# One more norm transposed by the DMA crossbar, and a new hand-written order, in a fused transformer block on one core

## The chip, the cores and the metric

The kernel runs on one core of one Trainium2 chip. The core has a matrix engine (TensorE, PE in the profile; PEld is its weight load), a vector engine (DVE), a scalar engine with activation tables (ACT), a general engine (POOL) and an engine used here to issue DMAs (SyncE, SP; SPq in the profile). The engines run side by side; each takes its own instructions strictly in order and waits on semaphores for data of the others. PSUM is the memory into which PE writes, SBUF the memory of everything else on the core. The metric is the device time of one launch in microseconds (us); lower is better. The profile is of one execution.

## The reference

One block of a transformer over 2048 tokens of width 512, all in bf16:

```python
mod = (silu(c) @ w_mod).reshape(1, 6, 1, 512)      # sa, ca, ga, sb, cb, gb
h = layernorm(x) * (1 + ca) + sa
q, k, v = heads(h @ wqkv)                          # 32 heads of 16
# each token attends to 8 tokens: itself and those 2, 4, ..., 14 before it
logits = einsum('bhsd,bhswd->bhsw', q, k[idx]) * 16 ** -0.5   # masked before token 0
o = einsum('bhsw,bhswd->bhsd', softmax(logits), v[idx])
x = x + ga * (o @ wo)
h = layernorm(x) * (1 + cb) + sb
x = x + gb * ((gelu(h @ w_gate) * (h @ w_up)) @ w_down)       # inner width 1792
```

## The kernel before

The tokens are cut into five groups: 0 and 1 have 256 tokens each, 2, 3 and 4 have 512. Each group passes through the same stages, and stages of different groups run side by side. In the profile they are known by these lines and names:

- First norm: DVE statistics (`st`, `mv`), the factor `rstd`, then `xn` (L532); a transpose puts the width on the partitions (`hT`); the modulation by `scl` and `modT` is applied after the transpose.
- qkv: PE, L673, `qkv_ps` from `hT` and `wq`, `wk`, `wv`; ACT copies the results to `qT`, `kT`, `vT` (L696). `vT` goes out to a DRAM scratch `scr` (L700) and comes back in shifted copies `vR` (L717).
- Attention: DVE multiplies q with shifted k (`pq`, L756), PE sums over the head (L768, into `LT`), ACT copies `LT` to `Lb` (L786), DVE takes a maximum in three steps (L789, L791, L793), PE subtracts it in PSUM (L798), ACT takes the exponential `e` (L805), PE sums (`ss`, L813), ACT inverts the sum by a logarithm and an exponential (L818, L819), DVE scales `e` (L822) and multiplies with `vR` (`pv`, L834 or L840), PE sums into `o_ps` (L853), ACT copies to `oT` (L859).
- Projection and second norm: PE `x_ps` (L878), DVE adds to x with a running sum (L882), ACT squares (L885), DVE and POOL make the factor `rstd` (L889, L891, L893, and the power at L537), DVE writes `xn` (L532), a transpose gives `h2T`.
- Feed-forward: PE `g_ps` and `u_ps` (L919), ACT the gelu `gl` (L928) and a copy `ub` (L931), DVE the product `hht` (L932), PE `y_ps` with the down weights `WdP` (L945), DVE adds (L953), SP stores (L956). `WdP` is multiplied by gb beforehand, in seven DVE operations (L973); `woP` by ga (L970).

A norm is transposed in one of two ways. Function `transposed` uses PE: eight 128x128 transposes for 256 tokens (L561, into PSUM `tp`), then four ACT operations that read PSUM, modulate, and write SBUF (L547). Function `crossbar` uses a transposing DMA from SBUF to SBUF, one for each 256 tokens (L583), issued by SP, and then four ACT operations that modulate in place (L593):

```python
        for half, xn in enumerate(xns):
            dma(262e3, lambda half=half, xn=xn: nc.sync.dma_start_transpose(
                out=dst[:, 2 * half:2 * half + 2, :, :].rearrange("p c d t -> p (c d) t"),
                in_=xn[:].rearrange("p i d -> p (i d)")), r=[xn], w=[(dst, ("half", half))], ...)
```

Two tables say which groups go which way: `XB1` for the first norm (group 4 by crossbar), `XB2` for the second (groups 2, 3 and 4).

The order of the work is not written out but planned when the kernel is built. Every stage records operations with an engine, an assumed duration, the tiles that they read and write, and a priority. Class `Plan` (`order`) then places one operation after another: of those whose inputs are placed it takes the one with the smallest pair of start time and priority, the start time being that at which the engine is free and the inputs have arrived, by the assumed durations. `PRI` holds the priorities: one per group for the stages ("ln1", "qkv", "att", "ffn", "glu"), one for each load ("load"), for the scratch stores and loads ("scr", "vR"), for the scaling of the weights ("wo", "wd") and the modulation rows ("mod"). `Plan.MARGIN` adds a time to an operation's start in this choice, per engine; `Plan.AHEAD` and `Plan.SKEW` say how early loads may be issued and how late they are assumed to land. These numbers decide nothing but the order of instructions on each engine.

Tiles come from rings of buffers. Those that matter here: four PSUM buffers (`psF`) for qkv, g, u and y; two (`psB`) for `x_ps`, `ss`, parts of `o_ps` and `tp`; two (`psL`) for `LT`; six for `pq` and `pv` together; three each for `gl` and `ub`; two each for `hT`, `h2T` and `vR`.

Of the kernel before, what the change touches and what calls it, by code (L numbers as in the profile page):

```python
# [184 lines left out]
class Engines:  # L185
    def __init__(self, nc, pl):
# [15 lines left out]
FMERGE = 0  # L202
CUT = 384
XB1 = {4: "act"}
XB2 = {2: "act", 3: "act", 4: "act"}
PRI = {
        "mod0": -90.9,
        "ln1": (-1628, -1309.8, -689.8, -49.3, 487.8),
        "qkv": (-615.4, 221.2, 164.3, 607.2, 1344.9),
        "att": (-458.5, 37.3, -1094.5, 559.4, 1849),  # L210
        "ffn": (1261.5, 2894.6, 2852.9, 2242.7, 1657.1),
        "glu": (-231.3, 441.7, -2194.3, 198.6, 1828.7),
        "mod": (-156.3, -280.2, 267.6),
        "wo": 978.5,
        "wd": 1221.7,
        "scr": -2870.3,
        "vR": -3349.8,
        "warm": (5, 7, 0, 3),
        "load": {"wv": -995.5, "x1": -998.36, "x2": -995.23, "wm2": -996.59, "wo": -880.76, "x3": -1009.12,
        "wm3": -995, "wm4": -996.09, "x4": -995.73, "Wg": -870.11, "Wu": -862.75, "wm5": -860.91, "Wd":  # L220
        -862.75},
}
Plan.MARGIN = {"pe": 0.45, "act": 0.17, "dve": 0.22, "pool": 0.29, "sp": -0.46}
Plan.AHEAD = 2.49
Plan.SKEW = 2
Plan.TURN = 0


# [1 line left out]
def kernel(  # L230
# [299 lines left out]
    def norm(tok, xn, i, mean, rstd, p):  # L530
        base = getattr(mean, "base", mean)
        dve(0.325, lambda: nc.vector.tensor_scalar(  # L532
            out=xn[:, i, :], in0=xrow(tok), scalar1=mean[:, i:i + 1], scalar2=rstd[:, i:i + 1], op0=ALU.subtract,
            op1=ALU.mult), r=[xkey(tok), (base, i), (rstd, i)], w=[(xn, i)], pri=p)
# [46 lines left out]
    def crossbar(xns, n, dst, off, p, on):  # L581
# [3 lines that stand above are left out]
                in_=xn[:].rearrange("p i d -> p (i d)")), r=[xn], w=[(dst, ("half", half))], pri=p, us=1.25, bw=290e3)  # L585
        for dt in range(DT):
            if on == "dve":
                dve(0.14 + n * 0.26e-3, lambda dt=dt: nc.vector.tensor_scalar(
                    out=dst[:, :, dt, :], in0=dst[:, :, dt, :], scalar1=scl[:, off // 2 + dt:off // 2 + dt + 1],
                    scalar2=modT[:, off + dt:off + dt + 1], op0=ALU.mult, op1=ALU.add),  # L590
                    r=[dst, (scl, off), (modT, off)], w=[(dst, dt)], pri=p)
            else:
                act(act_us(n, 2), lambda dt=dt: nc.scalar.activation(  # L593
                    out=dst[:, :, dt, :], in_=dst[:, :, dt, :], func=ACT.Identity,
                    scale=scl[:, off // 2 + dt:off // 2 + dt + 1], bias=modT[:, off + dt:off + dt + 1]),
                    r=[dst, (scl, off), (modT, off)], w=[(dst, dt)], pri=p)

    def columns(t, g, dt, xb):
        return t[:, :, dt, :] if g in xb else t[:, dt, 0:GROUPS[g][1]]

    def shaped(ap, g, xb):
        return ap.rearrange("p (c t) -> p c t", t=P) if g in xb else ap
# [103 lines left out]
    def emit_attention(g):  # L706
# [155 lines left out]
        lo = tok0 % SG if FMERGE else 0  # L862
        h2[g] = h2[g - 1] if lo else T("h2T", [P, n // P, DT, P] if g in XB2 else [P, DT, SG], BF16, "h2T")
        xns = []
        for half in range(n // 256):
# [31 lines left out]
            for i in range(2):  # L897
                norm(tok0 + 256 * half + P * i, xn, i, sx, rstd, p2)
        if g in XB2:
            crossbar(xns, n, h2[g], 8, base + 12, XB2[g])  # L900
        else:
            transposed(xns, n, h2[g], 8, base + 12, "ln2", ("psB", "psB"), False, lo)

    def emit_ffn(g):
# [4 lines left out]
        for u in range(units):  # L909
            p = PRI["ffn"][g] + u  # L910
            gu = []
            for Wt in (Wg, Wu):
                ps = T("psF", [P, nf, n], F32, "g_ps" if Wt is Wg else "u_ps", "ffn")

                def mm(Wt=Wt, ps=ps, u=u):
                    for f in range(nf):
                        ft = u * nf + f
                        for dt in range(DT):
                            nc.tensor.matmul(shaped(ps[:, f, :], g, XB2), lhsT=Wt[:, dt, ft * P:(ft + 1) * P],  # L919
                                             rhs=columns(h2[g], g, dt, XB2), start=(dt == 0), stop=(dt == DT - 1))  # L920

# [87 lines left out]
```

## Time and profile before

| | us |
|---|---|
| median of 4 runs (245.83 to 250.4) | 246.98 |
| the profiled execution, its own time | 246.29 |
| its span in the profile | 244.2 |
| PE busy | 236.3 |
| ACT busy | 159.9 |
| DVE busy | 158.5 |
| POOL busy | 15.7 |

The span is the time from the first to the last recorded instruction; 2.1 us of the execution's time lie around it. The busy times are sums over the span of the work of each engine. TensorE's granted clock is 0.993 over the span.

### The profile page before, as it was taken

To read this page: it belongs to the slowest core of one execution; us is meant where nothing else is said; L and a number is where in the kernel's file an instruction comes from. 1 tells how busy PE (TensorE), PEld (TensorE's weight loads), DVE (VectorE), ACT (ScalarE), POOL (GpSimd) and SP (SyncE) were. 2 spreads that over 40 slices of the span, in tenths; PEclk is the share of its full clock that TensorE was granted. 3 is DMA by queue.
4 is the path that set the end of the run, shared out by engine and by line. 5 is a ranking of instruction groups with operands and counts; after the bars stand their busy time and mean duration, and the time that the engine had idled before them with its cause. 6 is when DMAs were issued, how large, how long until landed. Compare 5 with 4: busy or idle time off the path is not lost.

```text
span 244.2 us, 4209 instructions
## 1 busy us (share of the span) xinstructions
PE 236.3 (97%) x1598; PEld 127.3 (52%) x1598; DVE 158.5 (65%) x302; ACT 159.9 (65%) x293; POOL 15.7 (6%) x37
## 2 busy tenths in 40 slices
PE   7899699999999999999999999999999999999995
PEld 2589455557675546675444444444444444444443
DVE  3569999639998699963699896369647222222222
ACT  5076897699887679478967675865767801666400
POOL 6002220100002000020000002000002000000000
PEclk9799999999999999999999999999999999999999
DMA  6999999999900129621108603101002200100011
GB/s 190 363 363 294 320 290 345 248 307 233 213 4 0 43 66 241 133 58 32 43 20 188 143 0 78 32 21 47 0 1 43 46 29 14 43 3 0 0 43 43
DMA packets 35477, 27.97 MB, mean 115 GB/s; under 512 B 9985, under 2 KB 34306, under 8 KB 35458
## 3 DMA queue, kind: packets, MB, share of 16 engines
q1 hardware_dynamic: 35456, 27.71, 44.0%
q8 instruction: 12, 0.20, 0.3%
q14 instruction: 7, 0.06, 0.1%
q10 hardware_dynamic: 2, 0.00, 0.0%
HBM read 21.40 MB, written 4.21 MB: 105 GB/s over the span
## 4 chain that ended last, share of the span: by engine, by line
PE 81%; DVE 9%; ACT 4%; DMA 2%; SPq 1%; POOL 1%; issue 1%; DVEq 0%; POOLq 0%
PE y_ps L945 18%; PE u_ps L919 18%; PE g_ps L919 18%; PE qkv_ps L673 14%; PE x_ps L878 5%; DVE pq L756 3%; PE o_ps L853 3%; DMA wm<-in_w_mod_dram 2%; DVE st L616 2%; PE LT L768 2%; ACT hT L593 1%; ACT hT L547 1%; PE LT L798 1%; POOL rstd L537 1%; DVE hht L932 1%; DVE xn L532 1%
## 5 line engine op out<-in xcount | busy, mean ns | idle before, releaser
L919 PE MATMUL u_ps<-h2T,Wu 128*128 128x512 bf16 (+1 forms) x280 | 57.7, 337 | 0.0
L919 PE MATMUL g_ps<-h2T,Wg 128*128 128x512 bf16 (+1 forms) x280 | 57.6, 336 | 0.0
L945 PE MATMUL y_ps<-WdP,hht 128*128 128x512 bf16 (+2 forms) x238 | 50.7, 367 | 0.0
L928 ACT ACTIVATE gl<-g_ps 128x512 bf16<-128x512 f32 x56 | 33.5, 599 | 22.7 <-PE g_ps L919 17.7
L932 DVE TENSOR_TENSOR hht<-gl,ub 128x512 bf16<-128x512 bf16 x56 | 23.5, 424 | 31.3 <-ACT ub L931 30.9
L931 ACT CAST ub<-u_ps 128x512 bf16<-128x512 f32 x56 | 32.7, 585 | 13.0 <-PE u_ps L919 12.7
L919 PEld LDWEIGHTS <-Wg 128*128 128x128 bf16 x280 | 27.2, 98 | 22.9 <-issue 0.6
L919 PEld LDWEIGHTS <-Wu 128*128 128x128 bf16 x280 | 27.0, 98 | 22.7 <-issue 2.1
L756 DVE TENSOR_TENSOR pq<-qT,kT 128x2048 bf16<-128x2048 bf16 x32 | 37.7, 1220 | 0.3 <-ACT kT L696 0.3
L945 PEld LDWEIGHTS <-hht 128*128 128x128 bf16 x238 | 22.7, 98 | 25.4 <-issue 0.4
L953 DVE TENSOR_TENSOR x_sg<-y_ps,x_sg 128x512 bf16<-128x512 f32 (+2 forms) x17 | 10.9, 658 | 27.3 <-PE y_ps L945 27.3
L834 DVE TENSOR_TENSOR pv<-e,vR 128x2048 bf16<-128x2048 bf16 x24 | 28.3, 1219 | 0.1
L537 POOL TENSOR_TENSOR rstd<-rstd,neghalf 128x2 f32<-128x2 f32 x14 | 11.5, 826 | 170.4 <-DVE rstd L893 106.1
L673 PE MATMUL qkv_ps<-hT,wq 128*128 128x512 bf16 (+1 forms) x80 | 17.8, 362 | 0.4 <-ACT hT L547 0.3
L673 PE MATMUL qkv_ps<-hT,wk 128*128 128x512 bf16 (+1 forms) x80 | 16.6, 340 | 0.0
L673 PE MATMUL qkv_ps<-hT,wv 128*128 128x512 bf16 (+1 forms) x80 | 15.2, 337 | 0.0
L878 PE MATMUL x_ps<-woP,oT 128*128 128x512 bf16 x64 | 15.1, 379 | 0.0
L885 ACT ACTIVATE xn<-x_sg 128x512 bf16<-128x512 bf16 x16 | 10.0, 626 | 6.9 <-DVE x_sg L882 6.7
L673 PEld LDWEIGHTS <-wq 128*128 128x128 bf16 x80 | 9.3, 119 | 6.2 <-issue 0.9
L882 DVE SCALAR_TENSOR_TENSOR x_sg<-x_ps,x_sg 128x512 bf16<-128x512 f32 x16 | 10.8, 689 | 2.2 <-PE x_ps L878 2.1
L696 ACT CAST qT<-qkv_ps 128x512 bf16<-128x512 f32 x16 | 9.4, 596 | 4.2 <-PE qkv_ps L673 4.1
L616 DVE BATCH_NORM_STATS2 st<-x_sg 128x6 f32<-128x512 bf16 x16 | 10.4, 682 | 2.5 <-DMA x_sg<-in_A_x_dram 2.5
(92 smaller groups left out, 214.6 us busy)
## 6 DMA issues: line engine op xcount, KB each, us to landing
vR<-scr SPq DMA_DIRECT2D x24, 260.0 KB, 5.3
vR<-scr SPq DMA_DIRECT2D x8, 264.0 KB, 9.3
wm<-in_w_mod_dram SPq DMA_DIRECT2D x8, 256.0 KB, 5.6
out_dram<-x_sg SPq DMA_DIRECT2D x15, 128.0 KB, 1.7
Wg<-in_B_w_gate_dram SPq DMA_DIRECT2D x2, 896.0 KB, 7.6
scr<-vT SPq DMA_DIRECT2D x7, 256.0 KB, 7.4
Wu<-in_B_w_up_dram SPq DMA_DIRECT2D x2, 896.0 KB, 12.4
WdP<-in_B_w_down_dram SPq DMA_DIRECT2D x2, 896.0 KB, 8.5
```

The costliest lines, as they stand in the source:

```text
L537: gp(0.75, lambda: nc.gpsimd.tensor_tensor(out=rstd[:], in0=rstd[:], in1=neghalf[:, 0:2], op=ALU.pow), r=[rstd, neghalf], w=[rstd], pri=p)
L616: dve(0.6, lambda i=i, st=st, tok=tok: nc.vector.bn_stats(out=st[:, i, :], in_=xrow(tok + P * i)), r=[xkey(tok + P * i)], w=[(st, i)], pri=p)
L673: nc.tensor.matmul(shaped(ps[:, jl, :], g, XB1), lhsT=wqkv[b][:, dt, j + jl:D:4], rhs=columns(hT[g], g, dt, XB1), start=(dt == 0 and (jl = ...
L756: dve(1.145, lambda j=j, wg=wg, no=no, t=pq[m]: nc.vector.tensor_tensor(out=t[:], in0=_ap(q[g][:, j, :], [[0, no], [1, n]]), in1=_ap(kT[:, ...
L834: dve(1.145, lambda jj=jj, jl=jl, wg=wg, t=pv[m]: nc.vector.tensor_tensor(out=t[:], in0=_ap(e[:, wg, :], [[0, 4], [1, n]]), in1=vR[g][jj][ ...
L878: nc.tensor.matmul(x1_ps[:], lhsT=oT[:, j, c4 * P:(c4 + 1) * P], rhs=woP[:, j, :], start=(j == 0), stop=(j == 3))
L919: nc.tensor.matmul(shaped(ps[:, f, :], g, XB2), lhsT=Wt[:, dt, ft * P:(ft + 1) * P], rhs=columns(h2[g], g, dt, XB2), start=(dt == 0), stop ...
L928: act(act_us(SG), lambda gl=gl, ps=gu[0]: nc.scalar.activation(out=gl[:], in_=flat(ps), func=ACT.Gelu_apprx_tanh), r=[gu[0]], w=[gl], pri= ...
L931: act(act_us(SG), lambda ub=ub, ps=gu[1]: nc.scalar.copy(out=ub[:], in_=flat(ps)), r=[gu[1]], w=[ub], pri=p)
L932: dve(0.339, lambda gl=gl, ub=ub, ht=hh[u // 2], u=u: nc.vector.tensor_tensor(out=ht[:, u % 2, :], in0=gl[:], in1=ub[:], op=ALU.mult), r=[ ...
L945: nc.tensor.matmul(y_ps[:], lhsT=hh[u // 2][:, u % 2, f * n + c4 * P:f * n + (c4 + 1) * P], rhs=WdP[:, ft, lo_d:hi_d], start=(ft == 0), st ...
L953: dve(0.07 + nd * 1.041e-3, lambda y_row=y_row, y_ps=y_ps: nc.vector.tensor_tensor(out=y_row(), in0=y_ps[:], in1=y_row(), op=ALU.add), r=[ ...
```

## The change

Group 1 is added to `XB2`: its second norm goes by `crossbar` and no longer by `transposed`. All priorities, the margins, `AHEAD` and `SKEW` get new values, and with them the order of instructions on each engine and of the DMAs in SP's queue.

```diff
 XB1 = {4: "act"}
-XB2 = {2: "act", 3: "act", 4: "act"}
+XB2 = {1: "act", 2: "act", 3: "act", 4: "act"}
 PRI = {
-        "mod0": -90.9,
-        "ln1": (-1628, -1309.8, -689.8, -49.3, 487.8),
-        "qkv": (-615.4, 221.2, 164.3, 607.2, 1344.9),
-        "att": (-458.5, 37.3, -1094.5, 559.4, 1849),
-        "ffn": (1261.5, 2894.6, 2852.9, 2242.7, 1657.1),
-        "glu": (-231.3, 441.7, -2194.3, 198.6, 1828.7),
-        "mod": (-156.3, -280.2, 267.6),
-        "wo": 978.5,
-        "wd": 1221.7,
-        "scr": -2870.3,
-        "vR": -3349.8,
+        "mod0": 24.6,
+        "ln1": (-1699.5, -1472.2, -535.1, -45.2, 539.7),
+        "qkv": (-614.8, 137.9, 320.7, 452.9, 1351.6),
+        "att": (-531.1, 91.8, -1108.7, 558.8, 1874.7),
+        "ffn": (1198.3, 2579.1, 2869.4, 2221.8, 1722.3),
+        "glu": (16.2, 624.6, -2193.8, 315.7, 1827.9),
+        "mod": (-276.9, -256.4, 195),
+        "wo": 1182.4,
+        "wd": 1255,
+        "scr": -3125.8,
+        "vR": -3434.5,
         "warm": (5, 7, 0, 3),
         "load": {"wv": -995.5, "x1": -998.36, "x2": -995.23, "wm2": -996.59, "wo": -880.76, "x3": -1009.12,
-        "wm3": -995, "wm4": -996.09, "x4": -995.73, "Wg": -870.11, "Wu": -862.75, "wm5": -860.91, "Wd":
+        "wm3": -994.66, "wm4": -984.59, "x4": -995.73, "Wg": -870.75, "Wu": -870.61, "wm5": -860.96, "Wd":
         -862.75},
 }
-Plan.MARGIN = {"pe": 0.45, "act": 0.17, "dve": 0.22, "pool": 0.29, "sp": -0.46}
-Plan.AHEAD = 2.49
-Plan.SKEW = 2
+Plan.MARGIN = {"pe": 0.49, "act": -0.1, "dve": 0.24, "pool": -0, "sp": 0.12}
+Plan.AHEAD = 1.76
+Plan.SKEW = 2.4
 Plan.TURN = 0
```

In the built kernels the first difference on PE lies in group 0's qkv (the transposes of group 1's first norm come ahead of all sixteen `wv` matmuls), the next ones around the projection of group 0, and most between the feed-forward of group 0 and that of group 3. From group 4's feed-forward on the order of PE is the same.

## The prediction

> **What bounds the kernel now.** I read the page's busy table first, then the waits of TensorE (PE), then the timelines of all engines around the places where the order changes.
>
> ```profile
> PE 236.3 (97%) x1598; PEld 127.3 (52%) x1598; DVE 158.5 (65%) x302; ACT 159.9 (65%) x293; POOL 15.7 (6%) x37
> ```
>
> ```profile
> PE LT L798 <- DVE Lb L793: 2.0, 1, 2.0
> PE warm_ps L452 <- DVE onecol L320: 1.3, 1, 1.3
> PE modT_ps L503 <- DMA wm<-in_w_mod_dram: 1.0, 2, 0.6
> PE qkv_ps L673 <- ACT hT L547: 0.3, 1, 0.3
> ```
>
> PE is busy 236.3 of 244.2 us. Its waits are 4.6 us, all before 36 us, and some 3 us follow its last matmul (final additions and stores). By the busy time per stretch, PE is idle 0.15 us from 36 us to its last matmul. So a step counts only if it removes PE work or a PE wait, or makes a new one. The time should move by the PE time removed plus whatever waits come or go.
>
> **Removed from PE.** The second norm of group 1 (tokens 256 to 511) is turned by eight 128x128 transposes in the timeline of PE:
>
> ```profile
> 73.89 2.75 PE L945 MATMUL y_ps<-WdP,hht 128*128 128x512 bf16 x12
> 76.79 0.60 PE L798 MATMUL LT<-Lb,NB 128*128 128x512 bf16 x2
> 77.23 0.61 PE L561 MATMUL tp<-ident,xn 128*128 128x128 bf16 x8
> 77.68 3.19 PE L945 MATMUL y_ps<-WdP,hht 128*128 128x512 bf16 x14
> 80.70 0.59 PE L813 MATMUL ss<-e,F 128*128 128x512 bf16 x2
> 81.13 0.59 PE L945 MATMUL y_ps<-WdP,hht 128*128 128x512 bf16 x2
> 81.56 1.03 PE L673 MATMUL qkv_ps<-hT,wq 128*128 128x512 bf16 x4
> ```
>
> Starts are what to read; durations overlap. The transposes hold PE from 77.23 to 77.68: **0.45 us**. The twelve y matmuls would take 12 x 0.216 = 2.59 (four follow each other in 0.863), to 76.48, but L798 starts at 76.79: it waits 0.31 for the last maximum (Lb L793). In the new order a wq block (0.86) goes ahead of the y matmuls, so PE reaches L798 at 73.89 + 0.86 + 2.59 = 77.34. By my working below Lb is ready at 76.5, and the **0.31** goes too. Then y x4, wk x4, y x8, ss, y x4: 77.34 + 0.43 + 0.86 + 0.86 + 1.73 + 0.43 + 0.86 = 82.5. Before, the same work without transposes (wq and wk follow 81.56) ends at 81.56 + 1.73 = 83.29. Sum: -0.77.
>
> **Added in its place.** One crossbar transpose on the queue of SyncE (SP) and four ACT modulations at L593 of 256 columns instead of four L547. Before shows no 256-column L593: bounds are 0.46 (spacing of the L547) and 0.81 (512 columns, L593). I take 0.48, nearest in size; the upper end adds 2 x 0.33 us ahead of the softmax's ss. How long a crossbar takes is in the table of DMA issues:
>
> ```profile
> h2T<-xn SPq DMA_TRANSPOSE x6, 3.0
> hT<-xn SPq DMA_TRANSPOSE x2, 6.9
> ```
>
> Six landed in 3.0 to 3.1 us on a quiet queue, two in 6.9 beside weight loads. From 73 to 80 us the slices show DMA nearly idle, so I take 3.0 and keep 6.9 as the end. The new waiter is ACT: its order there is exp x2, kT copy, two L593, both ss operations, two L593. Queued behind the first L593 is the softmax of group 2, for which DVE (pv) and then PE (o_ps) wait.
>
> [...]
>
> **DVE up to the transpose.** Rows used: pq 1.14, hht 0.34, WdP 0.60, x_sg 0.61 to 0.7, Lb steps 0.43, xn 0.33 each. Group 1's x projection now follows one more wk block, so its softmax runs 0.86 later and pv ends at 59.9 (before 59.0). PE has a g block moved ahead of that o_ps and comes at 61.1: covered by 1.1. Then pq x2 (62.2), hht x2 (62.9), pq x4 (67.4), hht x2 (68.1), pq x2 (70.4). PE needs those last two at 71.15: 0.6 spare. Then x_sg, hht, x_sg, WdP, WdP, hht (73.7), Lb, WdP, Lb, WdP (75.9), Lb (76.4), hht (76.7). PE needs the fourth WdP at 76.5 (0.5 spare) and Lb at 77.34 (0.9 spare). Then the norm, whose factor comes from GpSimd (POOL):
>
> ```profile
> 72.70 1.29 DVE L973 TENSOR_TENSOR WdP<-WdP,gbB 128x1024 bf16<-128x1024 bf16 x2
> ...
> 74.91 0.41 DVE L532 TENSOR_SCALAR xn<-x_sg,sx,rstd 128x512 bf16<-128x512 bf16 x1 [0.58 <-POOL rstd L537]
> ```
>
> That POOL power took 1.94 us, others 0.68 to 0.8; it ended only after DVE had fallen idle. I take the long one: factor at 77.3, xn at 78.05, crossbar landed at 81.2, two L593 to 82.2, both ss operations to 83.4 (before 82.52). DVE starts e at 83.5, pv at 84.75.
>
> **After the transpose.** Four pv end at 89.3; PE, after 82.5 + 6 x 0.864 + 2.59 + 0.1, wants them at 90.4 (spare 0.9 with the semaphore). A pq goes between pv 6 and 7, so the eighth ends at 95.05; PE moves two g/u pairs ahead and wants it at 95.9 (0.7). Six pq then hold DVE to 101.9, before x_sg and the first hht; three gl buffers fill, and the fourth gelu waits until 104.9. PE needs its PSUM buffer at 107.5 (2.1), and u's seventh buffer at 110.15 against 109.3 (0.8). Group 2's g starts at 117.9 against 118.64, its four L593 done at 116.9. So nothing gives the 0.77 back, but spares of 0.5 to 1 us are all there is.
>
> **Other moved steps.** All at nothing, each with its cover. The wv halves go behind two wm2 loads: 0.5 us of issue each, landing by about 14.6 (issue near 9.1 and 5.5), used from 15.3. All four woP loads go behind the first scr store: landed by 25, used by DVE at 31.3. The second Wu goes ahead of a WdP: used at 56 and 72. The second crossbar half of group 4's first norm goes behind two scr stores, which wait for vT at 57.0: issued 57.8, landed 60.8 to 64.7, ACT comes for it at 64.6. With vR for the last group swapped with scr: used 25 us later. The halo memsets on POOL move from 1.3 to about 5.5, used at 15. The new crossbar blocks SP from 62 to 78; behind it stand two output stores and vR loads that wait for pv at 89 anyway. The mask (L778) ahead of four transposes: ACT's copy of LT started at 25.11 behind another copy, so nothing. Groups 3 and 4 move their o_ps, x projection and LT blocks by up to two g/u blocks: the closest is group 3's o_ps, 0.86 earlier relative to L798, while ss and so pv come 1.0 earlier. If covers fail, each costs what it is late, at most some 1 us.
>
> **Sum.** 246.29 (the profiled execution: span 244.2 plus 2.1 around it) - 0.77 = 245.5. The median shown, 246.98, lies 0.7 above that execution, so I forecast 246.98 - 0.77 = **246.2**.
>
> **Rivals.**
> *The gain is absorbed (about 247.2).* DVE is busy 18.8 of the 20 us from 80 to 100. If DVE's chain runs 1.5 to 1.8 us later than I work out, for example through 0.66 from the upper L593 and some 1 us of POOL time or small gaps, o_ps of group 2 waits 0.8 to 1.1 and the gain is gone (+0.2). Against it: I already took the long POOL row. For it: many small spares in one chain.
> *The crossbar lands late (249.4, slower).* If it takes 6.9 instead of 3.0, ACT holds group 2's softmax 3.9 longer. 0.9 of it is spare; PE stands 3.0 at the first o_ps and 0.2 at the second: 246.2 + 3.2 = 249.4. It decides from a landing of about 3.9 us on, and costs more than the gain from 4.7. For it: the two 6.9 rows; against it: both were beside busy queues.
> *The wait of 2.0 at L798 goes as well (244.2).* Needs DVE's Lb steps at 26 to 28 us to come earlier. Against it: DVE's order there is the same, and it goes from operation to operation without waiting.
> *The change does nothing* is excluded: the built order has eight transposes fewer and one crossbar DMA more.
>
> **Numbers.** Forecast 0.52, absorbed 0.23, late crossbar 0.20, faster rival 0.05. What a measurement of this kernel can tell from no change is about 1%, 2.5 us: the four runs lie from 245.83 to 250.4. Faster by over 1%: the last rival, 0.05. Slower by over 1% (249.45): half of the late crossbar, and 0.05 out of the absorbed case for a queue that I read wrongly, 0.15. Within 1%: 0.80. Range: from 245.2 (the forecast less the 1 us by which the lowest run lies under the median) to 249.4.
>
> **What would show it.** Right: PE's busy time 0.4 to 0.5 lower, no L561 after 60 us, L798 near 77.3 without a wait, a crossbar landing in 3 us near 81, o_ps of group 2 without a wait near 90.4 and 95.9, the span near 243.4. Wrong: PE waiting at o_ps L853 for pv L834, ACT waiting at L593 for the DMA, or PE waiting for y's WdP near 76.

## The result, and the profile after

The changed kernel takes 245.25 us (median of 33 runs, 243.8 to 249.95), the kernel before 246.66 in the same comparison (54 runs). The medians differ by 1.4 us. The ratio is 0.9936, with a 95% interval of 0.9918 to 0.9954, that is 0.6% or 1.6 us faster; ratios here are taken without the few executions that ran slow as a whole, so they can differ a little from what the medians give. The forecast of 246.2 had the right sign, and the measured time lies inside its range, close to the lower end of 245.2; but the gain is about twice the 0.77 us that its sum had.

The profiled execution of the changed kernel took 244.13 us; its span is 242.1 us. The head of its page, and the waits of TensorE (waited in total, times, longest):

```profile
span 242.1 us, 4194 instructions
...
PE 233.6 (96%) x1590; PEld 126.0 (52%) x1590; DVE 158.3 (65%) x302; ACT 159.1 (66%) x293; POOL 15.0 (6%) x37
```

```profile
PE modT_ps L503 <- DMA wm<-in_w_mod_dram: 2.1, 3, 1.1
PE LT L798 <- DVE Lb L793: 1.7, 1, 1.7
PE warm_ps L452 <- DVE onecol L320: 1.3, 1, 1.3
PE qkv_ps L673 <- DMA wv<-in_A_wqkv_dram: 0.2, 1, 0.2
```

PE has eight matmuls fewer, as the change says. But its busy time fell by 2.7 us, not by 0.4 to 0.5, while its waits rose from 4.6 to 5.3 us. No wait lies after 36 us. The place where the transposes stood, in the timeline of PE (start, duration):

```profile
73.30 2.75 PE L945 MATMUL y_ps<-WdP,hht 128*128 128x512 bf16 x12
75.89 0.59 PE L798 MATMUL LT<-Lb,NB 128*128 128x512 bf16 x2
76.32 1.03 PE L945 MATMUL y_ps<-WdP,hht 128*128 128x512 bf16 x4
77.18 1.03 PE L673 MATMUL qkv_ps<-hT,wk 128*128 128x512 bf16 x4
78.05 1.89 PE L945 MATMUL y_ps<-WdP,hht 128*128 128x512 bf16 x8
79.77 0.59 PE L813 MATMUL ss<-e,F 128*128 128x512 bf16 x2
80.20 1.03 PE L945 MATMUL y_ps<-WdP,hht 128*128 128x512 bf16 x4
81.07 1.03 PE L673 MATMUL qkv_ps<-hT,wq 128*128 128x512 bf16 x4
```

The transposes are gone, and L798 follows the y matmuls without a wait. PE is through this work at 81.07. Before, the same work ended at 83.29: 2.22 us. Of these, 1.45 were there already at 54 us (group 0's first g_ps starts at 54.36, before at 55.81), and 0.77 arise here. Nothing is given back: group 2's g starts at 116.42, before at 118.64, again 2.22.

The 1.45 arise before 28 us. One row of the timeline shows where most of it lies, group 0's wq matmuls, first in the kernel before:

```profile
9.40 3.43 PE L673 MATMUL qkv_ps<-hT,wq 128*128 128x256 bf16 x16
```

and in the changed kernel:

```profile
9.44 1.92 PE L673 MATMUL qkv_ps<-hT,wq 128*128 128x256 bf16 x16
```

They are the same sixteen matmuls. In the execution of before the granted clock was 0.50 from 10 to 13 us; in that of after it was 1.00 throughout. So the two profiles differ by the granted clock too, and one pair of profiles can't say whether the change did that.

The crossbar, in the table of DMA issues of the changed kernel (median us to landing), is the quiet case, seven where six were:

```profile
h2T<-xn SPq DMA_TRANSPOSE x7, 3.1
hT<-xn SPq DMA_TRANSPOSE x2, 7.7
```

### The profile page after: what moved, and what is told of

It reads as the page before. It is cut to its first block, busy times and chain, and to the rows that moved or that the text cites. A ratio compares the mean times of both kernels' runs of the same rounds, so it can differ in the third digit from the quotient of the medians.

```text
span 242.1 us, 4194 instructions
## 1 busy us (share of the span) xinstructions
PE 233.6 (96%) x1590; PEld 126.0 (52%) x1590; DVE 158.3 (65%) x302; ACT 159.1 (66%) x293; POOL 15.0 (6%) x37
## 4 chain that ended last, share of the span: by engine, by line
PE 87%; DVE 6%; DMA 2%; ACT 2%; SPq 1%; issue 1%; DVEq 0%
PE g_ps L919 20%; PE u_ps L919 20%; PE y_ps L945 20%; PE qkv_ps L673 13%; PE x_ps L878 6%; PE o_ps L853 3%; PE LT L768 3%; DMA wm<-in_w_mod_dram 2%; DVE st L616 2%; DVE pq L756 2%; ACT hT L547 1%; PE LT L798 1%; PE ss L813 1%; SPq L415 1%; DVE x_sg L953 1%; DVE xn L532 1%
## 5 line engine op out<-in xcount | busy, mean ns | idle before, releaser
L537 POOL TENSOR_TENSOR rstd<-rstd,neghalf 128x2 f32<-128x2 f32 x14 | 10.6, 765 | 167.8 <-DVE rstd L893 106.7
L673 PE MATMUL qkv_ps<-hT,wq 128*128 128x512 bf16 (+1 forms) x80 | 16.3, 337 | 0.1
L673 PEld LDWEIGHTS <-wq 128*128 128x128 bf16 x80 | 8.7, 114 | 6.5 <-issue 2.4
L696 ACT CAST kT<-qkv_ps 128x512 bf16<-128x512 f32 x16 | 9.4, 591 | 3.9 <-PE qkv_ps L673 3.1
L673 PEld LDWEIGHTS <-wv 128*128 128x128 bf16 x80 | 8.7, 114 | 5.3 <-issue 0.6
```

The source lines that it names most:

```text
L537: gp(0.75, lambda: nc.gpsimd.tensor_tensor(out=rstd[:], in0=rstd[:], in1=neghalf[:, 0:2], op=ALU.pow), r=[rstd, neghalf], w=[rstd], pri=p)
L673: nc.tensor.matmul(shaped(ps[:, jl, :], g, XB1), lhsT=wqkv[b][:, dt, j + jl:D:4], rhs=columns(hT[g], g, dt, XB1), start=(dt == 0 and (jl = ...
```

## The clock of each execution

The granted clock over the span is known for each execution of the runs below and of the changed kernel, and it falls into four groups: 0.998 to 1.000 (called 1.000 from here on), 0.991 to 0.993, 0.984 to 0.986 and, seldom, 0.971 or 0.972. A lack of 0.007 is 1.7 us of a span of 244 us, which is what one stretch of some 3.4 us at half clock takes. The first profile of before has such a stretch: from 9 to 14 us its granted clock, us by us, is 0.80, 0.50, 0.50, 0.50 and 0.99. The share of executions, and their median, by clock (the kernel before over all comparisons below, on four chips, 157 of 158 executions; the changed kernel 33 of 34, from its own comparison; one of each at 0.97 is left out):

| granted clock | before: executions, us | changed: executions, us | difference |
|---|---|---|---|
| 1.000 | 30, 246.28 | 15, 244.14 | -2.1 |
| 0.991 to 0.993 | 90, 246.30 | 12, 245.31 | -1.0 |
| 0.984 to 0.986 | 37, 247.52 | 6, 246.93 | -0.6 |

The medians of before at 0.993 lie between 246.06 and 246.46 in the five comparisons, so differences of 0.2 mean nothing here. At one missing stretch the gain is near the predicted 0.77. Two things come on top. The changed kernel runs at full clock in 44% of its executions, the kernel before in 19%. And full clock is worth 1.2 us to the changed kernel, nothing to the kernel before by the medians; but its 30 executions at full clock are spread from 244.55 to 247.93, and eight of them took less than 245.5. The experiments ask what does each.

## The experiments

Times are medians against the kernel before on the same chip, in the same comparison; the chip differs between groups. Most kernels have twelve executions, so a single share of clocks is rough.

### What is chance, and which half of the change

**Before, unchanged.**

> The kernel before, unchanged, to see the granted clock of each of its runs. Work theory (the whole 1.57 us comes from less PE work and fewer waits): its fastest runs (245.6 to 245.9) have the granted clock 1.000, as the fastest runs of the changed kernel (243.8 to 244.5) do, so at equal clock the changed kernel is 1.7 to 1.8 us faster. Clock theory (about 0.77 us is work, the rest is that the changed kernel keeps the full TensorE clock in its first 20 us more often): no run of the kernel before, or almost none, has 1.000; its fastest have 0.993, like the changed kernel's runs at 245.0 to 245.7, and at equal clock the difference is 0.5 to 0.9 us.

Measured: 246.36 against 246.34, ratio 0.9982 (0.9953 to 1.0012). This is what no change looks like. Neither reading came true as written: three of the twelve ran at full clock, but at 245.59, 246.15 and 247.46 they were not the fast ones.

**The new order, transposes on PE.**

```diff
-XB2 = {1: "act", 2: "act", 3: "act", 4: "act"}
+XB2 = {2: "act", 3: "act", 4: "act"}
```

> The changed kernel with group 1's second norm back on TensorE and all the new priorities kept: the new order alone. Work theory of the prediction: eight transposes are 0.45 us, so it is 0.45 us slower than the changed kernel, about 245.7 (ratio 0.996 to 0.997 to the kernel before), the rest of the gain stays. Rival (the crossbar frees more than the transposes, for example ACT or PSUM): 1 us or more slower, 246.3 or above, ratio 0.999 or above. Clock theory: the share of runs at clock 1.000 stays that of the changed kernel, since the first 70 us are the same.

Measured: 245.46 against 246.34, ratio 0.9944 (0.9920 to 0.9967). Without the crossbar most of the gain is there. At equal clocks it is 0.5 to 0.6 above the changed kernel (245.80 against 245.31 at 0.993, 244.71 against 244.14 at 1.000): what the crossbar itself takes away, near the 0.45 of the eight transposes. Half of its executions, 6 of 12, ran at full clock.

**The crossbar, old priorities**, in the kernel before.

```diff
-XB2 = {2: "act", 3: "act", 4: "act"}
+XB2 = {1: "act", 2: "act", 3: "act", 4: "act"}
```

> The kernel before with group 1's second norm by the crossbar and all the old priorities: the crossbar alone (the planner still moves some steps behind it). Prediction's theory: 0.45 us faster than before by the transposes, up to 0.77 if the wait at L798 goes too: ratio 0.997 to 0.998. Rival (the new order is needed to hide the crossbar): no gain or slower, ratio 1.000 to 1.010, with ACT waiting for the DMA or PE at o_ps. Clock theory: granted clocks as the kernel before has them, since the first 70 us are the same.

Measured: 246.99 against 246.34, ratio 1.0006 (0.9982 to 1.0029): no gain. The timeline of PE shows why:

```profile
116.88 1.24 PE L311 MATMUL g_ps<-ident 128*128 128x512 bf16 x5
```

Five dummy matmuls, which neither kernel has. The planner can put them in (`filler`) where it expects TensorE to wait. They take 1.08 us.

**The same without the dummies.**

```diff
-                o.pads = max(0, min(16, int((at - came - self.SPARE) / self.PAD)))
+                o.pads = max(0, min(0, int((at - came - self.SPARE) / self.PAD)))
```

> Edit: the kernel before with group 1's second norm by the crossbar, as in the run of the crossbar alone, but without the five dummy matmuls (the planner's filler, at 116.9 us, 5 x 0.216 = 1.08 us) that the planner put ahead of a g block because it expected a wait there. Filler theory (the crossbar alone gains what it takes from TensorE, and the dummies ate it): 246.99 - 1.08 = 245.9, that is 0.4 to 0.5 under the kernel before. Absorbed theory (the dummies only stand where TensorE would have waited for h2T of group 2): 246.9 again, with a wait of about 1.1 us at L919 near 117 us.

Measured: 246.93 against 246.62, ratio 1.0021 (0.9990 to 1.0051). No gain either, so the dummies did not eat it. Two rows of the timeline of PE with a wait in brackets:

```profile
77.92 0.60 PE L798 MATMUL LT<-Lb,NB 128*128 128x512 bf16 x2 [0.63 <-DVE Lb L793]
...
120.63 0.38 PE L919 MATMUL g_ps<-h2T,Wg 128*128 128x512 bf16 x1 [0.49 <-ACT h2T L593]
```

TensorE comes 0.32 us earlier to L798 than DVE can follow (0.63 against the 0.31 of before), and 0.49 too early to group 2's g. The sum is -0.45 + 0.32 + 0.49 = +0.36; measured at a clock of 0.993: 246.74 against 246.30. These are waits of one execution (with the dummies, L798 waited 0.17). The crossbar alone gains nothing in the old order; that it needs the wq block ahead of the y matmuls, and what follows from it, is my reading of these waits, not a run of its own.

### Which part of the new order

The two plans agree in what is done by about 40 us. So the order can be cut there: the first part by one set of priorities, the rest by the other (`SWITCH` is 42 us on the planner's clock in the first run, 36 in the second).

```diff
+            late = engines.get("pe", 0.0) > self.SWITCH
+            margin = self.MARGIN2 if late else self.MARGIN
...
+            val = (lambda p: getattr(p, "b", p)) if late else float
...
-                key = (max(free, at + self.MARGIN[o.eng]) + turn, o.pri)
+                key = (max(free, at + margin[o.eng]) + turn, val(o.pri))
```

> Edit: the order of the kernel before, but with the new one's priorities until the planner's TensorE clock reaches 42 us; eight transposes of group 1's second norm stay on TensorE. DVE and ACT are as before; PE has group 1's first eight transposes ahead of the wv matmuls and the mask later, SP has both wv behind wm2, all woP behind the first scr store, the second Wu ahead of WdP. Split theory (the new order's first 42 us carry about half of the gain, by letting group 0's vR land earlier, so that an execution at full clock is no longer held at o_ps): median 245.6 to 245.8, that is 0.6 to 0.7 under the kernel before (246.34 in the last comparison); executions at a granted clock of 0.993 stay at 246.1, those at 1.000 come to 244.7 to 245.0 instead of 246.1 to 247.5. Late theory (all of the gain comes from 60 to 120 us): 246.35, no change. Clock theory (the new order leaves TensorE a shorter gap and so keeps its clock more often): nearly half of the executions at 1.000, as in the changed kernel (15 of 33), against 3 of 12 of the kernel before.

Measured: 245.86 against 246.62, ratio 0.9970 (0.9939 to 1.0001), 6 of 12 executions at 1.000.

> Edit: the other half: the old priorities until the planner's TensorE clock reaches 36 us, then the new ones, with group 1's second norm by the crossbar. Split theory: the 0.77 of the prediction alone, 245.6 median; at a clock of 0.993 the same 245.3 as the changed kernel, at 1.000 no better than 245 to 246.5, since vR still lands late. Late theory: all of it, 245.0 to 245.25. Clock theory: full clock as seldom as in the kernel before (about one in four or fewer), 245.6.

Measured: 245.53 against 246.62, ratio 0.9964 (0.9937 to 0.9992), one of 12 at 1.000. At 0.993 it takes 245.41, like the changed kernel (245.31) and 0.9 under the kernel before. So the late half is the predicted mechanism, at 0.9 where 0.77 was forecast. The early half is about as much again, and its sign is not certain from this run alone. The two halves add to more than the whole by the medians (0.76 and 1.09 against 1.4); the intervals are wide enough for that.

The traces separate the halves more sharply than the times do. From the start of group 0's first g_ps to the end of the last matmul of the kernel, TensorE takes:

| kernel | us |
|---|---|
| before, in both of its profiles | 185.42, 185.43 |
| the early half alone | 185.40 |
| the late half alone | 184.65 |
| changed | 184.65 |
| new order, transposes on PE | 185.09 |
| crossbar, old priorities, without dummies | 186.11 |

The late half is worth 0.77 whatever the clock of the execution: 0.33 of it the new order alone has, and the crossbar adds 0.44. The crossbar in the old order loses 0.69. All else that differs between the executions lies ahead of group 0's first g_ps, which starts between 54.14 and 57.20 us in the profiles of this case.

**The early DMA order alone.** PE, DVE, ACT and POOL keep their old order. `move` puts those of the loads that stand ahead of the named one right behind it: the first wv load behind both wm2 loads, the first woP load behind the first scr store, the first WdP load behind the second Wu load.

```diff
         placed = self.order()
+        has = lambda o, name: o.dma and any(t.name == name for t in o.tiles)
...
+        sp = lambda name: [o for o in placed if has(o, name)]
+        move(sp("wv"), sp("wm2")[-1])
+        move(sp("woP"), sp("scr")[0])
+        move(sp("WdP")[:1], sp("Wu")[-1])
```

> Edit: the kernel before with the early DMA order of the new one alone: both wv loads behind both wm2 loads, all woP behind the first scr store, the second Wu ahead of the first WdP; PE, DVE, ACT and POOL are in their old order. This is the run with the early half of the new order less the move of group 1's transposes, the mask and the halo memsets. If the DMA order is what raises the share of full clock (6 of 12 in that run, 1 to 3 of 12 with the old order) and gains 0.5: 245.9 again, about half at 1.000. If it is the place of group 1's eight transposes on PE: 246.35, 1 to 3 of 12 at 1.000, and o_ps waiting for pv where an execution does run at 1.000.

Measured: 245.59 against 246.49, ratio 0.9956 (0.9925 to 0.9987), 7 of 12 executions at 1.000, these at 244.84. TensorE's stretch from group 0's first g_ps on takes 185.42, as in the kernel before, so the gain lies ahead of it. So the early part of the gain needs neither the transposes of group 1's first norm nor the mask nor the memsets: the order of three pairs of DMAs gains as much without them.

Four runs with parts of it:

> Edit: the kernel before with one exchange on SP: the first woP load goes behind the first scr store, not ahead of it; all else is as before. Queue theory (this exchange is what lets vR land in time at full clock): executions at 1.000 at 244.7 to 245.2 without a wait of o_ps, those at 0.993 at 246.1 as before, median 246.0 to 246.3, and the share of full clock not changed. If it is the place of wv, or of the transposes, and not of woP: executions at 1.000 at 246 to 247.5 with o_ps waiting 1 to 2 us, as in the kernel before.

> Edit: the kernel before with one exchange on SP: the first wv load goes behind the two wm2 loads. If this is the part of the early DMA order that counts: 245.6 to 245.9, half of the executions at a granted clock of 1.000, those at 244.7 to 245. If it is the three together or another: 246.4, 1 to 3 of 12 at 1.000.

> Edit: the kernel before with the other two exchanges on SP: all woP behind the first scr store and the second Wu ahead of the first WdP, the wv loads in their old places. If wv counts: 246.4, as with woP alone. If it does not: 245.6 to 245.9.

> Edit: the kernel before with wv behind wm2 and woP behind the first scr store, Wu and WdP in their old places. If those two together are the early queue's part: 245.6. If Wu ahead of WdP is needed as well: 246.5.

Measured: woP alone 246.38 against 246.62 (0.9970 to 1.0029); wv alone 246.59 against 246.55 (0.9962 to 1.0014); all but wv 246.96 against 246.55 (0.9977 to 1.0029); wv and woP 246.15 against 246.36 (0.9961 to 1.0037). No single exchange gains, and woP alone, which I had taken for the cause, does not. The last run is inconclusive: 7 of 12 executions at full clock, at 245.03 in the middle, and the other five at 0.985. Whether Wu is needed too stays open.

### The clock, and what it is worth

**TensorE's first gap filled, in the changed kernel.** Seven dummy matmuls go into the waits for wm at 6 to 9 us.

```diff
+FILL = (0, 3, 2, 2)
...
                 for half in range(2):
+                    warm_mm(FILL[2 * i2 + half])
```

> The changed kernel with seven dummy matmuls (512 columns, results unused) put where PE waits for the modulation weights between 5.6 and 9.4 us: three, two and two. Clock theory: PE no longer falls quiet there, so the granted clock stays full and nearly all runs are at 1.000: about 244.0, ratio 0.988 to 0.990. Rival (the clock is lost elsewhere, or by chance): the same mix of clocks as the changed kernel, 245.0 to 245.6; or slower by up to 1 us where the dummies run at half clock and delay the modulation.

Measured: 245.85 against 246.34, ratio 0.9969 (0.9939 to 0.9998); 3 of 12 at 1.000, 6 at 0.993, 3 at 0.985. No help. In its profiled execution the clock held in the first gap and fell to half between 26 and 33 us (granted 0.82 from 24 to 28 us, 0.50 from 28 to 32, 0.83 from 32 to 36), at the wait of L798 (1.96 us, to 27.82). There are two places, then, and in this execution the second cost two stretches in a row. The profile of the run with the late half alone, granted 0.985, shows both in one execution, by the stretch (us, PE busy, then the granted clock):

```profile
9.00:13.00 4.00, 4.00 (x28) 0.63 1.09 376
24.00:34.00 10.00, 7.78 (x76) 0.83 1.12 281
```

**The second gap filled, then both.** Twelve matmuls of 256 columns ahead of group 0's L798, into the `ss` buffer that is not yet in use.

```diff
         def sub_max():
+            if tok0 == 0:
+                filler(ss.t, FILL2)
             for t in LT:
...
```

> Edit: the changed kernel with 12 dummy matmuls of 256 columns (12 x 0.11 = 1.3 us, into the unused ss buffer) ahead of group 0's first L798, where TensorE waits 1.7 us for the last maximum. Idle-gap theory (the granted clock falls to half for some 3.4 us after a stretch in which TensorE has little to do, and this gap is one of the two places): the stretch of half clock near 26 to 33 us is gone, executions at 0.985 become rare, the share at 1.000 rises from 15 of 33 to 8 or more of 12, median 244.1 to 244.6. Rival (what the matmuls are does not matter for the clock; the stretches come at times that no gap sets): share as before, median 245.3.

> Edit: both gaps of the changed kernel filled: the 7 dummy matmuls in the waits for wm at 6 to 9 us, as in the earlier run, and the 12 ahead of the first L798. Idle-gap theory: nearly all executions at 1.000, median 243.9 to 244.2. Rival: clocks spread over 0.985, 0.993 and 1.000 as in the run with the first gap filled (3, 6 and 3 of 12), median 245.5 to 245.9.

> Edit: the kernel before with both gaps filled in the same way. Idle-gap theory together with the queue theory (at full clock the old order is held by group 0's vR, which lands late): nearly all executions at 1.000, but at 245.2 to 247.5, no better than now, with o_ps waiting for pv up to 2 us at 38 to 42 us; median 245.5 to 246.5. If vR holds nothing: 244.9, as the executions at full clock should be 1.4 below those at 0.993. Rival of the clock: 246.4 as before.

> Edit: the kernel before with the early DMA order of the new one and with both gaps filled by dummy matmuls; it completes a square with the kernel before (246.49), the fill alone (246.37, all 12 at 1.000) and the queue alone (245.59, 7 of 12 at 1.000). Queue theory (at full clock the old order is held by the landing of group 0's vR, the new one less so): all at 1.000, 244.7 to 245.0. If the queue only raises the share of full clock, and does nothing for vR: 246.4, as with the fill alone.

| kernel | gaps | executions at 1.000 | us (before) | ratio, interval |
|---|---|---|---|---|
| changed | second filled | 4 of 6, the others 0.993 | 244.47 (246.49) | 0.9897 (0.9862 to 0.9933) |
| changed | both filled | 7 of 7 | 244.65 (246.49) | 0.9914 (0.9879 to 0.9949) |
| before | both filled | 12 of 12 | 246.37 (246.49) | 0.9973 (0.9945 to 1.0001) |
| before, new early DMA order | open | 7 of 12 | 245.59 (246.49) | 0.9956 (0.9925 to 0.9987) |
| before, new early DMA order | both filled | 12 of 12 | 245.45 (246.55) | 0.9958 (0.9934 to 0.9981) |

With both gaps filled all 31 executions ran at 0.998 or more, and so did the five of one more kernel below; with both open it was 15 of 34 of the changed kernel and 30 of 158 of the kernel before. So, by intervention, work of TensorE at these two places keeps the clock of these kernels. And holding the clock is worth little in the old order, 246.37 filled against 246.49 open; the interval allows at most 0.6%. The early DMA order is worth 0.9 us with the gaps open and 1.1 with them filled, or 0.9 against the kernel before with its gaps filled, which ran in another comparison (246.37). Two runs stayed behind what was expected: the changed kernel with both gaps filled (243.9 to 244.2 expected) and the early DMA order with both filled (244.7 to 245.0 expected). In the profiles of both, o_ps waited 0.7 for pv, and DVE 3.35 and 3.84 for vR.

What can make full clock worth nothing: the repeated run of the kernel before was profiled in an execution at full clock, the slowest of its three (247.46). Its timeline of DVE, at the first multiplication by vR:

```profile
38.27 4.63 DVE L840 TENSOR_TENSOR pv<-e,vR 128x2048 bf16<-128x2048 bf16 x4 [5.14 <-DMA vR<-scr]
```

and, of the same execution, the longest entry in the waits of PE:

```profile
PE o_ps L853 <- DVE pv L840: 1.9, 3, 0.7
```

TensorE came to o_ps 1.75 us earlier than in the first profile (39.83 against 41.58), DVE stood 5.14 us for vR, and TensorE gave the time back at o_ps. In the changed kernel at full clock, the same row of DVE:

```profile
36.09 4.63 DVE L840 TENSOR_TENSOR pv<-e,vR 128x2048 bf16<-128x2048 bf16 x4 [2.54 <-DMA vR<-scr]
```

2.2 us earlier, just in time for o_ps at 40.09. SP issued the scr store at 16.93 and vR at 22.84 there; in the repeated run of before at 17.42, behind a woP issue that held SP for 2.71, and at 25.75.

This pair must not be taken for the difference between the two orders. In three other profiles of the old DMA order at full clock that woP issue took 1.38 to 1.42 us, and vR lands early or late in either order. First the kernel before with both gaps filled, in an execution of 245.01, then the early DMA order with both gaps filled, in one of 247.40:

```profile
35.71 4.63 DVE L845 TENSOR_TENSOR pv<-e,vR 128x2048 bf16<-128x2048 bf16 x4 [2.08 <-DMA vR<-scr]
...
38.21 4.63 DVE L859 TENSOR_TENSOR pv<-e,vR 128x2048 bf16<-128x2048 bf16 x4 [3.84 <-DMA vR<-scr]
```

All profiles at full clock in which PE has its old early order:

| run | DMA order | first pv by vR | first g_ps | us |
|---|---|---|---|---|
| before, filled | old | 35.71 | 54.42 | 245.01 |
| crossbar with dummies | old | 35.78 | 54.48 | 245.68 |
| crossbar without dummies | old | 37.75 | 56.46 | 247.70 |
| before, repeated | old | 38.27 | 56.98 | 247.46 |
| wv and woP | part | 35.08 | 54.33 | 244.82 |
| early DMA order | new | 35.73 | 54.44 | 244.93 |
| early DMA order, filled | new | 38.21 | 56.92 | 247.40 |

But for the one with wv and woP, where vR came earliest, group 0's first g_ps starts 18.70 or 18.71 us after the first pv. So in these six it is the landing of vR that sets the time, and it varies by 2.5 us between them. That the new DMA order makes an early landing more frequent is what the medians say (245.45 against 246.37, all at full clock); single profiles don't show it, as both orders have early and late ones. At half clock a late vR is covered: in the profile of the run with woP alone, granted 0.986, the first pv started at 38.19, and o_ps, which came at 42.92, did not wait.

### Is the landing of vR all that is left?

The loads of Wg (1.8 MB) stand ahead of vR in SP's queue. They are first used at 54 us. Moved behind vR, with both gaps filled and with both open:

```diff
         placed = self.order()
...
+        move(sp("Wg"), sp("vR")[3])
```

> Edit: the changed kernel with both gaps filled, and with both Wg loads (1.8 MB) behind group 0's four vR loads in SP's queue, not ahead of them. If the transfer of Wg is what vR waits behind: vR lands about 3 us earlier, DVE's wait for it (3.3 us) and that of o_ps (0.7) go, median 243.9 instead of 244.65, executions near each other. If vR is held by the landing of its own scr store, or by its own many small packets: 244.6, with the wait of 3 us as before. If Wg is then late: a wait of the first g_ps near 54 us.

> Edit: the changed kernel with both Wg loads behind group 0's four vR loads, no dummy matmuls. If vR is what holds the changed kernel at full clock: its executions at 1.000 come from 243.8 to 245.9 down to 243.7 to 244.0, those at 0.993 stay at 245.3, median 244.5 to 245.2 as the shares fall. If the held clock did it in the run with both: 245.2, as the changed kernel.

Measured with the gaps filled: 244.05 against 246.55 (5 executions, 243.82 to 244.61), ratio 0.9886 (0.9856 to 0.9916). DVE's row, without a wait:

```profile
33.28 4.63 DVE L857 TENSOR_TENSOR pv<-e,vR 128x2048 bf16<-128x2048 bf16 x4
```

vR came at least 3.3 us earlier than with the gaps filled alone, whose pv started at 36.60 after a wait of 3.35 and made o_ps wait 0.7. Its five executions lie within 0.8 us, the seven of that run within 1.8. This version beats both kernels. With the gaps open: 245.27 against 246.36, ratio 0.9942 (0.9912 to 0.9973); three executions at 1.000 take 243.96 to 244.06, eight at 0.991 to 0.993 take 245.32 in the middle. That is the changed kernel again. At 0.993 the earlier vR is worth nothing (245.32 against 245.31); at full clock it is 0.1 with the gaps open (244.00 against 244.14) and 0.6 with them filled (244.05 against 244.65).

## Why the prediction was half right

**Right: the late half, term by term in the profiles.** The transposes (0.45) and the wait at group 2's L798 (0.31) went, and TensorE's lead grows by 0.77 between 54 and 81 us. The runs give both terms apart: 0.33 by the order alone, 0.44 more by the crossbar. Corrected by the lead of 1.45 that was there before, the starts come out: L798 forecast 77.34 less 1.45 is 75.89, and it is 75.89; pv 84.75 less 1.45 is 83.30, and it is 83.29; the two o_ps 90.4 and 95.9 less 1.45 are 88.95 and 94.45, and they are 88.93 and 94.39. The run with the late half alone confirms it in time: 0.9 at equal clock.

**Right with time to spare: the crossbar's way.** POOL's power took 1.00 us, not 1.94, and xn was ready at 76.00, earlier than I had it (78.05 less 1.45 is 76.60). The crossbar landed 3.1 us after its issue at 76.04, some 0.6 us ahead of the forecast (81.2 less 1.45); ACT waited 0.31 for it and did an L593 in 0.59 (spacing 0.5), near the 0.48 taken, and then waited 0.17 for PE's ss, so it held nothing up.

**The rivals.** The late crossbar (6.9 us) did not occur: its rows stay with the two transposes of the first norm, beside other loads (7.7 in the changed kernel, at a DMA share of 1.13 from 48 to 55 us and 1.18 from 56 to 64; from 76 to 80 us, at the new one, it was 0.34). The absorbed gain did not occur either, but it is what the crossbar does in the old order: DVE's chain is late at L798, and g waits for h2T. The rival in which the first L798's wait of 2.0 goes did not happen (1.7 remain), yet what the sum lacked arose in the same part of the kernel, ahead of group 0's first g_ps.

**Wrong: the step "Other moved steps. All at nothing".** The early DMAs were priced at nothing, each by when it is used itself (wv at 15.3, woP at 31.3). The cover of woP held (issued by 19.63, 5.6 us to landing, used at 29.83); wv was wanted 1.4 us earlier at full clock and made TensorE wait 0.2. What I did not follow is who is queued behind them on SP: the scr store and, behind its landing, vR. The profile of before did not show this: its TensorE ran at half clock from 10 to 13 us and came to o_ps at 41.58, and in that execution the first pv had started at 35.30, after a wait of 0.3 for vR. I took that execution's clock of 0.993 as a property of the kernel; the clock differs from execution to execution, and the gain with it. The runs put the early DMA order at 0.9 to 1.1 us, in place of my zero; that this comes by way of vR is argued from the full-clock profiles, and not traced from the order itself. The rest of the distance from 246.2 to 245.25, 0.3 us, is the median of before, 246.98 by four runs and 246.66 by 54.

**Open.** Why the early DMA order also raises the share of full clock. Over all runs without fillers it is 44 of 94 executions with wv behind wm2 and woP behind scr together, against 41 of 230 with one or neither of them. The gaps that decide it are the same two, but no profile shows what the queue changes in them. And vR lands up to 2.5 us earlier or later from one execution to the next in the same order, while exchanges that do nothing one by one gain 0.9 to 1.1 together; which packets stand before which was not traced.

## What to carry to other kernels

Before a profile is used as the baseline of a sum, ask which parts of it belong to that execution: here a stretch at half clock covered a wait that decided at full clock (a first pv at 38.19 cost nothing at 0.986, one at 38.27 made o_ps wait 1.9 at 1.000). When a DMA is moved in a queue, the price is not only whether it lands in time itself, but which store and which dependent load stand behind it: with Wg moved behind vR the first pv started at 33.28, with Wg ahead at 36.60. And ask of a transpose moved off a busy engine whether the engine's next inputs come earlier by as much; here the crossbar gained 0.4 to 0.5 us in the new order and nothing in the old, where TensorE waited 0.32 more at L798 and 0.49 for h2T.

## What I had not expected of the hardware

- Gaps well below the length of the half-clock stretch (some 3.4 us) cost it. In four profiles whose clock, by the stretch, fell at the first place (before, the early half, the late half, woP alone) TensorE's longest single wait there was 0.6 to 0.9 us, among short and narrow matmuls; in four in which it fell at the second (transposes on PE, first gap filled, the late half, woP alone) it was 1.7 to 2.0. The changed kernel's profile passed waits of 1.1 and 1.7 at full clock, so the length alone does not decide. With dummy matmuls at both places 36 of 36 executions ran at 0.998 or more.
- The same kernel shows none, one or two such stretches from one execution to the next: of 158 executions of the kernel before, 30 ran at 1.000, 90 at 0.991 to 0.993, 37 at 0.984 to 0.986 and one at 0.971, steps of 0.007 of 244 us, that is 1.7 us, half of 3.4. What decides it in a single execution was not shown.
- Moving 1.8 MB of weights behind four loads of 264 KB made those usable at least 3.3 us earlier, by one profile of each (first pv at 33.28 against 36.60), without making the weights late: TensorE waited for none of them.
